# Making all of w_out's factors inside the h stage of the second MoE, and other due times for the attention steps, in a fused attention and two-MoE kernel on one Trainium2 core

## The chip, the cores and the metric

The kernel runs on one core of one Trainium2 chip, as one launch. The time is in device microseconds (us). The engines are TensorE (PE, matmuls; PEld is its weight load), VectorE (DVE), ScalarE (ACT), GpSimd (POOL) and SyncE (SP), which here issues every transfer. Each engine works through its own list of instructions in order. When an instruction waits, everything behind it on that engine waits too.

## The reference, cut to what matters

```python
q, k, v: (4, 8, 576, 64)            # batch, heads, sequence, head size
scores = where(mask, q @ k.T / 8, -1e9)   # heads 0-3: the last 32 keys; heads 4-7: every 32nd key
x  = softmax(scores) @ v                  # -> 2304 tokens x 512
h  = x @ w_in                             # first MoE, 512 -> 2048
x2 = (h * sigmoid(1.702 * h)) @ w_out     # 2048 -> 512
h2 = x2 @ w_in2                           # second MoE
out = (h2 * sigmoid(h2)) @ w_out2         # 2304 x 512
```

All inputs and the output are float32.

## The kernel before, in words

**Tiling.** The 2304 tokens are 8 chunks of 288 (half a sequence each). For every chunk there is an attention, then an h run of 16 groups (one for each 128 columns of w_in; a group is 12 matmuls of 288 columns), a gelu on each, then a g run of 16 groups of the same size against w_out. Matmuls are in fp16. Each float32 operand is split in a high and a low half, and a product takes three matmuls (high-high, high-low, low-high). Splitting takes two instructions: ACT or POOL writes the high half, and DVE's scalar_tensor_tensor then writes the low one.

**The second MoE** uses a Strassen-like form with 7 products in place of 8 for each pair of 2x2 blocks. It runs on whole pieces of 512 tokens (four, and one of 256), first all of h2 = x2 @ w_in2 ("the h stage", 18 blocks of 7 products, PE lines L1183), then the output ("the out stage", 18 blocks, L1294). For this both weight matrices have to be turned into 7 forms, called factors. w_in2 and w_out2 each give 8 batches. A batch loads two 128x512 tiles (A and B) from a scratch in HBM, makes two tiles U and V from them with four adds of 128x256, and splits the results in high and low halves: 5 high halves and 5 low halves for w_out2.

**Two planners.** Each instruction (or a short group) is a task with engines that may run it, a due time (its priority, in planned us) and buffers that it takes from named pools. A list scheduler in Python runs the tasks on modelled costs and writes down the resulting order for each engine. So a due time is no time on the chip: it decides the order on the queues, and nothing else. The first planner covers all but the last chunk; `PERIOD = 57` planned us separate chunk starts. The second covers chunk 7 (its h and g runs, L1013 and L1032), the h stage and the out stage.

**The attention of chunk c** runs within chunk c-1. `ATT` gives the due time of each step from that chunk's start: loads of q and v; sums of squares for the scale; the scale; the splits of q, k and v; then four head pairs (`s` for the first, `step` between them): scores on PE (L654 and L673), row maxima on DVE (L682), exps on ACT (L701), the normalising products on POOL (L719), transposes on PE (L726), their split (ACT L739, DVE L743); and last the products with v (`av`, L775) and the split of x (ACT L805, DVE L808). The gelu of the h run (L865) and the exp (L701) need different tables in ACT, so each change from one to the other loads a table.

**w_in2's factors** (`factors(0, i, ...)`, 8 batches) are made within the first planner, due at 245 + 22 i, and are stored to the scratch `in_factors`; the second planner loads them into the tile wf. **w_out2's factors** are made in two places. Three batches (`WO_EARLY`) come in the first planner, due at 415 + 20 i. Five come in chunk 7, due at 4 + 7 i (`factors_out`). All are stored to the scratch `out_factors` (L542, L1112) from buffers of the pool "f", and loaded from there during the h stage into regA and regB (L1120), where the out stage reads them. The pool "f" of the second planner has four buffers. It also serves each h block for the three factors that the block makes of its own result (L985) and stores with the rest of h2 (L1200, scratch `g_scratch`).

**An h block** runs 7 products into four PSUM banks of eight; ACT copies the first bank out (L1214) and applies silu to the second (L1223). DVE adds the other five results (L1190), ACT applies silu to those (L1195), and POOL or DVE makes the three factors (L985). L1214 of a block waits for the factors of the block two before it. The x2 pieces are loaded (L1144, L1146), added (L985) and split (L980 or L982, L992) in the same way, one piece ahead.

Helpers that all of this passes through have one line each: L385 and L387 (high halves, ACT and POOL) and L392 (low halves) in the first planner, L980, L982 and L992 in the second, L507 for the batch adds of the first planner, L295 and L290 for converting the parked weights.

## Time and profile before

| | us |
|---|---|
| median of 3 runs | 906.48 (902.98 to 908.37) |
| the profiled execution | 902.06 |
| its span on the core | 899.9 |
| PE busy in the span | 855.9 (95%) |
| DVE, ACT, POOL busy | 673.0, 591.0, 415.6 |
| HBM read and written | 107.74 MB and 60.82 MB |

The profiled execution is one run with the hardware profiler, and its own time is 2.2 us above its span. PE is busy for 95% of the span, so the time that an engine other than PE spends matters only where PE waits for it. The whole of PE's idle time is 44 us.

### The profile page before, as it was taken

How to read it: one execution, taken by the hardware profiler on the slowest of the kernel's cores; microseconds unless marked ns; L12 is line 12 of the kernel's file. 1: busy time of each engine (PE TensorE's matmuls, PEld its weight loads, DVE VectorE, ACT ScalarE, POOL GpSimd, SP SyncE). 2: the span in 40 equal slices, each digit the busy share in tenths (PEclk: the TensorE clock that was granted, in tenths of full speed). 3: DMA queues.
4: the chain of work that ended last, by engine and by line, in shares of the span. 5: the costliest groups of instructions: out<-in, count | busy, mean ns of one | idle time of the engine just before them, and what ended most of it. 6: DMA issues, size and time to landing. Idle time of an engine off the chain costs nothing.

```text
span 899.9 us, 21584 instructions
## 1 busy us (share of the span) xinstructions
PE 855.9 (95%) x8198; PEld 722.9 (80%) x8198; DVE 673.0 (75%) x1208; ACT 591.0 (66%) x1406; POOL 415.6 (46%) x426
## 2 busy tenths in 40 slices
PE   5999887999999899989999999989999999999997
PEld 4877675787887787777788788878888998888886
DVE  3799788987758788988668396768666489977852
ACT  5789588999969978879779464344444377555430
POOL 4667564453431445656337285556555242312110
PEclk9999999999999999999999999999999999999999
DMA  9857342464337376456413396888786669765611
GB/s 314 263 168 229 107 128 96 128 180 171 104 100 224 102 223 197 134 169 190 137 60 113 112 395 220 259 302 273 261 279 224 206 228 310 249 217 181 213 41 47
DMA packets 101319, 169.96 MB, mean 189 GB/s; under 512 B 9312, under 2 KB 58976, under 8 KB 100192
## 3 DMA queue, kind: packets, MB, share of 16 engines
q1 hardware_dynamic: 101216, 168.60, 57.9%
q8 instruction: 64, 1.05, 0.5%
q14 instruction: 39, 0.32, 0.1%
HBM read 107.74 MB, written 60.82 MB: 187 GB/s over the span
## 4 chain that ended last, share of the span: by engine, by line
PE 66%; DVE 13%; ACT 11%; DMA 4%; issue 3%; POOL 3%; SPq 0%; DVEq 0%; POOLq 0%; ACTq 0%
PE aps L1183 9%; PE aps L1294 9%; PE hps L1183 5%; PE gps L1183 4%; PE gps L888 4%; PE gps L1294 4%; PE hps L1294 3%; PE aps L857 3%; PE hps L888 3%; PE aps L888 3%; ACT sms L701 2%; ACT sml L701 2%; PE gps L857 2%; PE hps L857 2%; DVE wm L290 1%
## 5 line engine op out<-in xcount | busy, mean ns | idle before, releaser
L1183 PEld LDWEIGHTS <-wf 128*128 128x128 f16 x1680 | 151.2, 98 | 20.4 <-issue 4.5
L1294 PEld LDWEIGHTS <-wf 128*128 128x128 f16 x1512 | 147.8, 98 | 19.1 <-issue 1.6
L857 PEld LDWEIGHTS <-regA 128*128 128x128 f16 x1152 | 112.9, 99 | 41.8 <-issue 10.3
L985 POOL TENSOR_TENSOR tt<-tt 128x256 f32<-128x256 f32 (+2 forms) x102 | 89.0, 889 | 100.7 <-ACT tt L1195 22.0
L888 PEld LDWEIGHTS <-regB 128*128 128x128 f16 x1152 | 109.1, 98 | 29.0 <-issue 2.1
L857 PE MATMUL aps<-x,regA 128*128 128x288 f16 x576 | 76.8, 286 | 2.3 <-DVE g L392 1.4
L295 POOL TENSOR_TENSOR wm<-wm 128x512 int32<-128x512 int32 x32 | 42.5, 1328 | 69.2 <-DVE wm L290 40.0
L980 ACT ACTIVATE wf<-tt,xsg 128x512 f16<-128x512 f32 x86 | 56.9, 712 | 22.3 <-DMA tt<-g_scratch 8.5
L1294 PE MATMUL aps<-regA,wf 128*128 128x256 f16 x600 | 68.3, 273 | 1.4 <-DVE tt L1309 0.9
L992 DVE SCALAR_TENSOR_TENSOR wf<-tt,xsg,wf 128x512 f16<-128x512 f32 x86 | 68.5, 844 | 0.0
L719 POOL TENSOR_TENSOR sml<-sml,sus 96x384 f32<-96x384 f32 x32 | 30.3, 947 | 66.1 <-DVE sus L710 49.6
L888 PE MATMUL aps<-g,regB 128*128 128x288 f16 x432 | 58.1, 286 | 1.4 <-ACT sml L701 1.4
L1195 ACT ACTIVATE tt<-tt 128x512 f32<-128x512 f32 x35 | 22.0, 629 | 47.5 <-DVE tt L1190 42.7
L888 PE MATMUL gps<-g,regB 128*128 128x288 f16 x384 | 51.5, 286 | 0.8 <-ACT sms L701 0.8
L857 PE MATMUL gps<-x,regA 128*128 128x288 f16 x324 | 45.5, 292 | 7.0 <-DVE g L392 5.9
L1183 PE MATMUL aps<-xfa,wf 128*128 128x256 f16 (+1 forms) x444 | 46.6, 262 | 4.3 <-DVE x L1190 4.3
L888 PE MATMUL hps<-g,regB 128*128 128x288 f16 x336 | 45.7, 286 | 0.0
L539 DVE SCALAR_TENSOR_TENSOR wm<-wm,s 128x512 f16<-128x512 f32 (+1 forms) x47 | 41.0, 888 | 3.9 <-POOL wm L387 2.9
L1183 PE MATMUL aps<-g,wf 128*128 128x256 f16 x360 | 42.7, 273 | 0.0
L387 POOL TENSOR_SCALAR wm<-wm,s 128x512 f16<-128x512 f32 (+1 forms) x31 | 25.6, 833 | 25.5 <-issue 10.2
L980 ACT ACTIVATE wf<-regB,xsg 128x512 f16<-128x512 f32 x40 | 27.4, 712 | 13.7 <-PE hps L1294 3.8
L857 PE MATMUL hps<-x,regA 128*128 128x288 f16 x252 | 34.1, 286 | 1.6 <-DVE wm L290 1.6
(368 smaller groups left out, 2157.1 us busy)
## 6 DMA issues: line engine op xcount, KB each, us to landing
tt<-g_scratch SPq DMA_DIRECT2D x72, 256.0 KB, 4.0
g_scratch<-tt SPq DMA_DIRECT2D x62, 256.0 KB, 3.0
w<-in_moe_w_out_dram SPq DMA_DIRECT2D x24, 512.0 KB, 3.7
regB<-g_scratch SPq DMA_DIRECT2D x36, 256.0 KB, 4.2
rv<-in_v_dram SPq DMA_DIRECT2D x8, 1024.0 KB, 5.1
regB<-in_moe_w_in_dram SPq DMA_DIRECT2D x16, 512.0 KB, 8.2
w<-in_moe_w_in_dram SPq DMA_DIRECT2D x16, 512.0 KB, 3.7
w_scratch<-wm SPq DMA_DIRECT2D x32, 256.0 KB, 2.8
```

Of the source, the lines that this page charges most:

```text
L295: nc.gpsimd.tensor_tensor(out=di, in0=m.bitcast(I32), in1=di, op=ALU.add)
L387: nc.gpsimd.tensor_scalar(out=out, in0=in_, scalar1=s, scalar2=1.0, op0=ALU.mult, op1=ALU.mult)
L539: k = P.add(dve_t(256 * w), prio, lambda on, O=O, src=src: nc.vector.scalar_tensor_tensor(out=O()[:, 1], in0=src(), scalar=sc[nm][0], in1= ...
L701: nc.scalar.activation(out=sm[0:nq, e * nk:e * nk + nk], in_=bank[0:nq, (e % 4) * nk:(e % 4) * nk + nk], func=AF.Exp, bias=nms[0:nq, sl.id ...
L719: nc.gpsimd.tensor_tensor(out=smv(), in0=smv(), in1=sus[0:nq, sl.idx, 3 * g:3 * g + nb, None].to_broadcast([nq, nb, nk]), op=ALU.mult), [k ...
L857: nc.tensor.matmul(o, lhsT=pvA[:, f, x, kk, :], rhs=x1[:, y, kk, :], start=(i == 0), stop=(i == 3 * KD - 1))
L888: nc.tensor.matmul(o, lhsT=pvB[:, f, u, dt * 128:(dt + 1) * 128], rhs=g1[:, w, f, :], start=(f == 0 and j == 0), stop=(f == KF - 1 and j = ...
L980: nc.scalar.activation(out=out, in_=in_, func=AF.Copy, scale=s)
L985: return P.add({e: x for e, x in any_add(n).items() if e in by}, prio, lambda on: (nc.gpsimd if on == "POOL" else nc.vector).tensor_tensor ...
L992: dve_t(n), prio, lambda on: nc.vector.scalar_tensor_tensor(out=lo(), in0=src(), scalar=s(), in1=hi(), op0=ALU.mult, op1=ALU.subtract),
L1183: nc.tensor.matmul(place(b, f), lhsT=wf[:, nf * g + f, x, wa, 128 * kk:128 * kk + 128], rhs=rhs.rearrange("p (h t) -> p h t", h=2) if n2 = ...
L1294: nc.tensor.matmul(bank(b)[:, 256 * half:256 * half + 256], lhsT=fb[:, x, a, 128 * f:128 * f + 128], rhs=wt[:, 4 * p + f, z, wi, :], start ...
```

## The change

All 8 batches of w_out2's factors are made by the second planner in the h stage, one each 18 planned us, and their halves are written straight into regA and regB; `out_factors` and its stores and loads are gone. Each batch takes the four buffers of a new pool "w" (the former pool "r", in regB's rear, free once chunk 7's g run has read regB). These four go on to the out stage's pool "y" only after the last batch, where the pool "r" went there at the end of chunk 7. The batches of w_in2 come each 26 planned us in place of 22. And the attention steps of chunks 2 to 7 are due 8 planned us earlier, with 6 us in place of 5 between head pairs, and 4 to 5 us earlier for the products with v.

```diff
-FACT = ((245.0, 22.0), (415.0, 20.0))
-WO_EARLY = 3
-WO_LATE = (4.0, 7.0)
+FACT = (250.0, 26.0)
...
-ATT = {"load": (-20.0, -13.0), "square": (-8.0, 0.0), "scale": 2.0, "split": (6.0, 7.0, 16.0), "s": 22.0, "step": 5.0,
-       "av": (36.0, 49.0)}
+ATT = {"load": (-28.0, -20.0), "square": (-16.0, -8.0), "scale": -6.0, "split": (-2.0, 0.0, 10.0), "s": 14.0, "step": 6.0,
+       "av": (32.0, 44.0)}
...
-    for n, dst in enumerate((wfs, wos)):
-        for i in range(KF // 2 if n == 0 else WO_EARLY):
-            factors(n, i, FACT[n][0] + FACT[n][1] * i, k_w2[n], dst)
+    for i in range(KF // 2):
+        factors(i, FACT[0] + FACT[1] * i, k_w2[0])
...
     def factors_out(i, prio):
 
-        a, b, u, v = (P.buf("t") for _ in range(4))
+        a, b, u, v = (P.buf("w") for _ in range(4))
...
-        ka = P.dma(prio - 8, 0.25, lambda on: nc.sync.dma_start(out=A(), in_=w2s[1, i]), [x for z in late[:-1][-1:] for x in z], [a, u, v])
+        ka = P.dma(prio - 8, 0.25, lambda on: nc.sync.dma_start(out=A(), in_=w2s[1, i]), g_mm, [a, b, u, v], at=prio - 10)
...
-            o = P.buf("f")
-            O = lambda o=o, w=w: sl(o).bitcast(F16).rearrange("p (h e) -> p h e", h=2)[:, :, 0:256 * w]
-            h = P.add(any_hi(256 * w), prio, lambda on, O=O, src=src: put(on, O()[:, 0], src(), sc["wo"][0]), deps, [o], [x])
-            k = P.add(dve_t(256 * w), prio, lambda on, O=O, src=src: nc.vector.scalar_tensor_tensor(
-                out=O()[:, 1], in0=src(), scalar=sc["wo"][0], in1=O()[:, 0], op0=ALU.mult, op1=ALU.subtract),
-                [h], (), [x, o], two=True)
-            k_out[i].append(P.dma(prio + 2, 0.125 * w, lambda on, O=O, m=m, w=w: nc.sync.dma_start(
-                out=wos[i, :, :, m:m + w, :].rearrange("p h m e -> p h (m e)"), in_=O()), [k], (), [o]))
...
+            w = [lambda h=h, t=t, m=m, n=n: t[:, i, h, m:m + n, :].rearrange("p m e -> p (m e)") for h in range(2)]
+            out.append(halves(prio, 256 * n, w[0], w[1], src, lambda: sc["wo"][0], deps, [x]))
+        return out
+
+    wo = [factors_out(i, B0 + 14 + 18 * i) for i in range(8)]
...
-    P.add({"SP": 0.0}, 1e6, lambda on: None, g_mm, [P.buf("r", "y") for _ in range(4)])
+    P.add({"SP": 0.0}, 1e6, lambda on: None, g_mm, [P.buf("r", "w") for _ in range(4)])
+    P.add({"SP": 0.0}, 1e6, lambda on: None, [k for x in wo for k in x], [P.buf("w", "y") for _ in range(4)])
```

`B0` is the planned end of chunk 7, and `g_mm` its last g groups.

What the change moves on the queues is read from the order of the instructions. Lines after the change stand a little lower: L1188, L1197, L1169, L968, L1174, L1118, L1120 and L1026 are the old L1214, L1223, L1195, L980, L1200, L1144, L1146 and L1038; in the first planner L854, L690, L383, L820, L429 and L281 are L865, L701, L385, L831, L431 and L283.

**ACT, at the start of the h stage, before.** `tt<-tt,s` are high halves of the last two w_out2 batches, `g_78<-tt,s` those of an x2 piece.

```order
L1214 ACTIVATE tt<-aps,xih_6622 128x512
L980 ACTIVATE tt<-tt,s 128x256
L1214 ACTIVATE tt<-aps,xih_6622 128x512
L980 ACTIVATE g_78<-tt,s 128x512
L980 ACTIVATE g_78<-tt,s 128x256
L980 ACTIVATE tt<-tt,s 128x256 x2
L1223 ACT_TABLE_LOAD
L1223 ACTIVATE tt<-aps,xih_6622 128x512 x2
```

The same place after the change, where `regA<-regB,s` are high halves of the first w_out2 batch:

```order
L1188 ACTIVATE tt<-aps,xih_6559 128x512
L968 ACTIVATE g_78<-tt,s 128x512
L1188 ACTIVATE tt<-aps,xih_6559 128x512
L968 ACTIVATE g_78<-tt,s 128x512
L968 ACTIVATE regA<-regB,s 128x256
L968 ACTIVATE g_78<-tt,s 128x512
L968 ACTIVATE regA<-regB,s 128x512
L1169 ACT_TABLE_LOAD
```

The halves that have to wait for a buffer of the pool "f" are gone from between L1214 and the silus; halves of a batch still stand there, and now write where nothing has to be stored first.

**SP, at the start of the h stage, before.** `g_scratch<-` are the stores of h2.

```order
L1112 DMA out_factors<-tt 256x1x256 x2
L1200 DMA g_scratch<-tt 128x256
L1112 DMA out_factors<-tt 256x1x512
L1112 DMA out_factors<-tt 256x1x256
L1200 DMA g_scratch<-tt 128x256
L1112 DMA out_factors<-tt 256x1x512
L1112 DMA out_factors<-tt 256x1x256
L1200 DMA g_scratch<-tt 128x2x256 x2
L1120 DMA regA<-out_factors 128x2x1024
```

SP after the change, where `regB<-w_scratch` are a batch's two loads into the pool "w":

```order
L1118 DMA tt<-x_scratch 128x512
L1081 DMA regB<-w_scratch 128x512
L1120 DMA tt<-x_scratch 128x512
L1082 DMA regB<-w_scratch 128x512
L1174 DMA g_scratch<-tt 128x2x256
L1174 DMA g_scratch<-tt 128x256 x2
L1174 DMA g_scratch<-tt 128x2x256 x2
...
L1174 DMA g_scratch<-g_78 128x2x256
L1081 DMA regB<-w_scratch 128x512
```

No factor store stands among the h2 stores; instead the two loads of each later batch stand among them, and the first of the two waits there until the batch before it has left the pool "w".

**ACT, where chunk 4's g run passes into chunk 5's h run, before.** `g_78<-gps,sg` are high halves of a gelu, `wm<-wm,s` those of a w_in2 batch.

```order
L385 ACTIVATE wm<-wm,s 128x512
L865 ACT_TABLE_LOAD
L865 ACTIVATE gps<-gps,invh 128x288
L831 ACTIVATE ts<-hps,invg 128x288
L385 ACTIVATE g_78<-gps,sg 128x288
L865 ACTIVATE gps<-gps,invh 128x288
L701 ACT_TABLE_LOAD
L701 ACTIVATE sml,sus<-hps,nms,sc 96x128
L385 ACTIVATE g_78<-gps,sg 128x288
L431 ACTIVATE wm<-w_110 128x512
L865 ACT_TABLE_LOAD
```

The same place after:

```order
L690 ACTIVATE sml,sus<-gps,nms,sc 96x128 x3
L690 ACTIVATE sms,sus<-gps,nms,sc 72x72 x4
L854 ACT_TABLE_LOAD
L854 ACTIVATE aps<-aps,invh 128x288 x2
L383 ACTIVATE g_78<-aps,sg 128x288 x2
L429 ACTIVATE wm<-w_110 128x512
L854 ACTIVATE hps<-hps,invh 128x288
L281 ACTIVATE wm<-w_110 128x512
L383 ACTIVATE g_78<-hps,sg 128x288
L820 ACTIVATE ts<-hps,invg 128x288
```

The last exps of the attention now come before the first gelu, with one table load in place of three, and the batch halves stand elsewhere. Over the whole list up to chunk 7, ACT has 25 loads of the exp and gelu tables in place of 29.

## Rows read from the trace of the kernel before

**Rows 1.** The page, busy us of each engine, its share of the span, instructions.

```profile
PE 855.9 (95%) x8198; PEld 722.9 (80%) x8198; DVE 673.0 (75%) x1208; ACT 591.0 (66%) x1406; POOL 415.6 (46%) x426
```

**Rows 2.** Windows by stage: length, busy PE, PEld, DVE, ACT, POOL, clock, DMA.

```profile
137.30:205.40 68.10, 61.05 (x587) 48.58 (x587) 60.06 (x114) 61.39 (x162) 31.73 (x29) 0.97 0.44 137
205.40:509.60 304.20, 293.87 (x3118) 240.16 (x3116) 231.68 (x478) 248.05 (x672) 138.77 (x134) 1.00 0.47 145
509.60:556.80 47.20, 47.20 (x388) 37.73 (x387) 36.08 (x61) 24.16 (x50) 33.20 (x42) 1.00 0.87 314
556.80:725.60 168.80, 164.52 (x1636) 148.44 (x1634) 112.98 (x176) 70.62 (x119) 86.62 (x113) 0.99 0.75 246
725.60:899.90 174.30, 168.42 (x1564) 150.46 (x1561) 127.73 (x192) 84.74 (x136) 41.67 (x23) 1.00 0.57 189
```

**Rows 3.** Timeline of PE: start, length, instruction, in brackets idle before and releaser.

```profile
145.25 3.03 PE L857 MATMUL gps<-x,regA 128*128 128x288 f16 x12 [2.71 <-DVE g L392]
...
297.54 0.44 PE L726 MATMUL hps<-idt,sml 96*128 96x96 f32 x3 [1.42 <-DVE ptt L743]
...
397.32 1.63 PE L857 MATMUL gps<-x,regA 128*128 128x288 f16 x12 [1.20 <-DVE g L392]
...
400.25 1.63 PE L857 MATMUL gps<-x,regA 128*128 128x288 f16 x12 [1.29 <-DVE g L392]
...
430.61 0.76 PE L775 MATMUL hps<-ptt,vz 128*128 128x96 f16 x14 [0.96 <-DVE ptt L743]
...
588.90 2.72 PE L1183 MATMUL aps<-xfa,wf 128*128 128x256 f16 x12 [4.28 <-DVE x L1190]
591.41 1.70 PE L1183 MATMUL gps<-g,wf 128*128 128x256 f16 x12
...
752.01 1.47 PE L1294 MATMUL aps<-regA,wf 128*128 128x256 f16 x12 [0.92 <-DVE tt L1309]
```

**Rows 4.** Timelines of ACT, POOL and DVE ahead of PE's wait at 588.90.

```profile
569.91 0.51 ACT L980 ACTIVATE tt<-tt,s 128x256 f16<-128x256 f32 x1 [6.83 <-DMA out_factors<-tt]
...
577.48 7.30 POOL L985 TENSOR_TENSOR tt<-tt 128x256 f32<-128x256 f32 x8 [3.35 <-DMA out_factors<-tt]
...
585.09 0.72 ACT L980 ACTIVATE g<-tt,s 128x512 f16<-128x512 f32 x1 [2.96 <-DVE tt L985]
...
585.85 2.33 DVE L992 SCALAR_TENSOR_TENSOR g<-tt,s,g 128x512 f16<-128x512 f32 x2
...
586.64 1.25 ACT L1214 ACTIVATE tt<-aps,xih 128x512 f32<-128x512 f32 x2
...
588.11 0.74 DVE L1190 SCALAR_TENSOR_TENSOR x<-aps,xih,tt 128x512 f32<-128x512 f32 x1
```

**Rows 5.** DMA issues: transfer, count, size each, median us to landing.

```profile
tt<-w_scratch SPq DMA_DIRECT2D x9, 256.0 KB, 4.6
...
out_factors<-tt SPq DMA_DIRECT2D x15, 128.0 KB, 4.8
```

**Rows 6.** Timelines of POOL and ACT ahead of PE's waits at 397.32 and 400.25.

```profile
386.06 7.31 POOL L507 TENSOR_TENSOR wm<-wm 128x256 f32<-128x256 f32 x4
...
393.40 0.72 ACT L385 ACTIVATE wm<-wm,s 128x512 f16<-128x512 f32 x1 [2.81 <-POOL wm L507]
...
397.10 1.28 ACT L701 ACT_TABLE_LOAD   x1
```

**Rows 7.** Windows of line L1109 alone: length, busy DVE (instructions), clock, DMA.

```profile
509.60:556.80 47.20, 12.49 (x15) 1.00 0.87 314
...
556.80:725.60 168.80, 6.60 (x10) 0.99 0.75 246
```

**Rows 8.** Line L1109: count, shortest, median and longest in ns, first and last start, shapes.

```profile
L1109 DVE SCALAR_TENSOR_TENSOR tt<-tt,s x21: 473/745/1214, 515.5 to 570.5; 128x256 f16<-128x256 f32 x13, 128x512 f16<-128x512 f32 x8
```

**Rows 9.** Groups of instructions from 509 to 580: count, busy us, mean ns, idle before.

```profile
L985 POOL TENSOR_TENSOR tt<-tt 128x256 f32<-128x256 f32 x26 | 22.7, 894 | 26.3 <-DMA tt<-w_scratch 15.6 <-DMA out_factors<-tt 3.3 <-DMA tt<-x_scratch 3.0
...
L980 ACT ACTIVATE tt<-tt,s 128x512 f16<-128x512 f32 x5 | 3.5, 709 | 0.0
```

More of the change, by code (lines that the diff above doesn't have):

```diff
@@ L220, in attention_moe_moe2_kernel @@
     x2s = nc.dram_tensor("x2_scratch", (KD, 128, NT), F32, kind="Internal").ap()
-    wfs, wos = (nc.dram_tensor(f"{nm}_factors", (KF // 2, 128, 2, 7, 256), F16, kind="Internal").ap() for nm in ("in", "out"))
+    wfs = nc.dram_tensor("in_factors", (KF // 2, 128, 2, 7, 256), F16, kind="Internal").ap()
     w2s = nc.dram_tensor("w2_scratch", (2, KF, 128, 512), F32, kind="Internal").ap()
@@ L510, in attention_moe_moe2_kernel, with factors @@
     fed = [None]
[L512 to L514 removed]
+    def factors(i, prio, k_s):
         a, b, u, v = (P.buf("f") for _ in range(4))
         A, B, U, V = (lambda x=x: wm[:, x.idx] for x in (a, b, u, v))
[L517 to L518 removed]
+        ka = P.dma(prio - 8, 0.25, lambda on: nc.sync.dma_start(out=A(), in_=w2s[0, i]), [k_s, k_parked[0, i], fed[0]], [a, b], at=prio - 12)
+        kb = P.dma(prio - 8, 0.25, lambda on: nc.sync.dma_start(out=B(), in_=w2s[0, i + 8]), [ka, k_parked[0, i + 8]], (), [b])
         lo = lambda X: lambda: X()[:, 0:256]
         hi = lambda X: lambda: X()[:, 256:512]
[L521 to L533 removed]
+        k1 = any_add(prio, lo(U), lo(B), hi(B), ALU.add, [kb], [u, v], [b])
+        k3 = any_add(prio, lo(V), lo(A), lo(B), ALU.subtract, [ka, kb, k1], (), [v, a, b])
+        k2 = any_add(prio, hi(U), lo(U), lo(A), ALU.subtract, [k1, ka], (), [u, a])
+        k4 = any_add(prio, hi(V), hi(A), hi(U), ALU.subtract, [k2, k3], (), [v, a, u])
+        parts = ((a, A, 0, 2, [ka]), (b, hi(B), 2, 1, [kb]), (u, U, 3, 2, [k1, k2]), (v, V, 5, 2, [k3, k4]))
         fed[0] = k1
@@ L1088, in attention_moe_moe2_kernel @@
         out=wf[:, i].rearrange("p h m e -> p (h m e)"), in_=wfs[i].rearrange("p h m e -> p (h m e)")), at=4.5 * i)] for i in range(8)]
-    k_out, late = {}, []
     def factors_out(i, prio):
-        a, b, u, v = (P.buf("t") for _ in range(4))
+        a, b, u, v = (P.buf("w") for _ in range(4))
         A, B, U, V = (lambda x=x: sl(x) for x in (a, b, u, v))
-        ka = P.dma(prio - 8, 0.25, lambda on: nc.sync.dma_start(out=A(), in_=w2s[1, i]), [x for z in late[:-1][-1:] for x in z], [a, u, v])
-        kb = P.dma(prio - 8, 0.25, lambda on: nc.sync.dma_start(out=B(), in_=w2s[1, i + 8]), [x for z in late[:-1][-1:] for x in z], [b])
+        ka = P.dma(prio - 8, 0.25, lambda on: nc.sync.dma_start(out=A(), in_=w2s[1, i]), g_mm, [a, b, u, v], at=prio - 10)
@@ L1097, in factors_out @@
+        kb = P.dma(prio - 8, 0.25, lambda on: nc.sync.dma_start(out=B(), in_=w2s[1, i + 8]), [ka], (), [b])
         lo = lambda X: lambda: X()[:, LO]
         hi = lambda X: lambda: X()[:, HI]
-        k1 = add_up(prio, 256, lo(U), hi(A), lo(A), ALU.subtract, [ka], (), [u, v, a])
-        k3 = add_up(prio, 256, lo(V), hi(B), hi(A), ALU.subtract, [k1, kb], (), [v, a, b])
+        k1 = add_up(prio, 256, lo(U), hi(A), lo(A), ALU.subtract, [ka], (), [u, a])
+        k3 = add_up(prio, 256, lo(V), hi(B), hi(A), ALU.subtract, [ka, kb], (), [v, a, b])
@@ L1115, in attention_moe_moe2_kernel @@
-    for i in range(WO_EARLY, 8):
-        factors_out(i, WO_LATE[0] + WO_LATE[1] * (i - WO_EARLY))
-        late.append(k_out[i])
-    wo = []
-    for i in range(8):
-        wo.append([P.dma(B0 + 20 + 15 * i + e, 0.46, lambda on, i=i, w=w, m=m: nc.sync.dma_start(
-            out=w[:, i].rearrange("p h m d -> p h (m d)"), in_=wos[i, :, :, m].rearrange("p h m d -> p h (m d)")), [*g_mm, *k_out.get(i, [])], at=B0 + 5 + 15 * i)
-            for e, (w, m) in enumerate(((woa, slice(0, 4)), (wob, slice(4, 7))))])
+        out = []
@@ new lines, in factors_out @@
+        for x, src, t, m, n, deps in ((a, lo(A), woa, 0, 1, [ka]), (b, B, woa, 1, 2, [kb]), (v, lo(V), woa, 3, 1, [k3]),
+                                      (u, U, wob, 0, 2, [k1, k2]), (v, hi(V), wob, 2, 1, [k4])):
+            w = [lambda h=h, t=t, m=m, n=n: t[:, i, h, m:m + n, :].rearrange("p m e -> p (m e)") for h in range(2)]
+            out.append(halves(prio, 256 * n, w[0], w[1], src, lambda: sc["wo"][0], deps, [x]))
+        return out
+    wo = [factors_out(i, B0 + 14 + 18 * i) for i in range(8)]
```

28 lines of the change are left out of this document (4 added, 24 removed).

## The prediction

> **What bounds the kernel now.** I read the page first: PE is busy for 855.9 of 899.9 us [rows 1], so the whole kernel follows PE, and what a change off PE can win or lose is a share of the 44 us in which PE is idle. The windows by stage say where these lie [rows 2]. The stretch of chunk 1's attention and h run loses 68.10 - 61.05 = 7.05 us, the five chunks after it 304.20 - 293.87 = 10.33, chunk 7 nothing, the h stage 168.80 - 164.52 = 4.28, the out stage 5.9. The rest, 16.5 us, is the start, which the change does not reach. In the same rows DVE is the next engine: 60.06 of 68.10 in the first stretch, 231.68 of 304.20 in the chunks, 112.98 of 168.80 in the h stage.
>
> Then the timeline of PE, for the waits themselves [rows 3]. The h stage's whole loss is one wait: 4.28 us before 588.90, for an L1190 of DVE. The matmuls behind it are slow too: 2.72 us for twelve that take 1.47 elsewhere, then 1.70. The chunks lose in many small pieces: twice a gelu half (L392), twice the split of transposed scores (L743), 0.96 to 1.42 us each. Of each wait I looked at what stood ahead of its releaser on the other engines.
>
> For 588.90 that is plain [rows 4]. ACT stood for 6.83 us until 569.91, because a high half of a late w_out2 batch had no buffer: the store of an earlier half had not landed. POOL stood for 3.35 us until 577.48 for the same kind of store, and did eight adds after that. So the block factors and an x2 piece came late, ACT waited 2.96 us more for that piece, its L1214 went out at 586.64, and DVE's L1190 behind two L992 at 588.11; PE began 0.8 us later. A store of this kind takes 4.8 us to land [rows 5], and four buffers serve these stores and the h blocks.
>
> For 397.32 and 400.25 it is a batch of w_in2's factors [rows 6]: four adds on POOL took 7.31 us from 386.06, ACT stood 2.81 us for one of them with a high half at the head of its queue, and the first gelu of chunk 5, the change of table and the first gelu halves all stood behind it. Right after, at 397.10, ACT changed its table back for one exp, 1.28 us.
>
> **The change part by part.** The sum is made against the profiled execution's own 902.06 us, which is 4.4 us (0.5%) below the median of 906.48; at the end I scale by the ratio.
>
> *The late batches leave chunk 7.* PE has no idle time there [rows 2], so their 12.49 us of DVE in chunk 7 and 6.60 in the first blocks [rows 7] are worth nothing in themselves. Worth something is that no store of theirs holds a buffer of the pool "f" any more. With it goes the wait of 4.28 us, and the slow matmuls behind it: 2.72 - 1.47 = 1.25 and 1.70 - 1.47 = 0.23. Together -5.76 us. The bounds are 0 (another delay of the same blocks takes its place) and -5.76; I take all of it, since both waits that began the chain name these stores. What is late next is the first w_out2 batch. Its loads can go out only when chunk 7's g run is done with regB; one takes 4.6 us [rows 5], and its first half stands behind the second block's L1214, some 9 us on, so they are covered.
>
> *Eight batches enter the h stage.* Five late batches cost DVE 12.49 + 6.60 = 19.09 us of low halves [rows 7], so 3.82 each and 30.5 for eight. DVE then has 112.98 - 6.60 + 30.5 = 136.9 us in a stage of 164.5 (83%). ACT gets at most 32 high halves at 0.709 [rows 9], 22.7 us on 70.62, and POOL 27 adds at 0.894, 24.1 on 86.62. None is full: the cover is PE itself, and the out stage runs with 127.73 of DVE in 174.30 with a largest wait of 0.92 us in the rows shown [rows 2, 3]. What remains is order: a high half waits at the head of ACT for a POOL add, and L1214, L1223 and the silus wait behind it. That is the mechanism of 397.32. It cost PE 1.20 + 1.29 = 2.49 us in one of eleven batches of the first planner, 0.23 us a batch, so I take 8 x 0.23 = +1.8 us. The bounds are 0 and 8 x 2.49 = 19.9.
>
> *SP.* 40 stores and 16 loads go, 16 loads from w_scratch stay. A batch's first load waits on SP until the batch before has left its buffers, with h2 stores behind it; if a batch is late by some us, these stores are too, and with them buffers of "f". That is the same price as above by another door, and I keep it in the same bounds. The out stage's first loads can use regB's rear only after the last batch; they find the x2 pieces' buffers first, so I cost it at nothing; without that cover it is one load, 4.6 us by the nearest row [rows 5].
>
> *Attention due 8 earlier, and eight batches in place of eleven in the chunks.* The instructions stay the same but for four table loads (5.1 us of ACT at 1.28 [rows 6]) and the three batches, 3 x 3.82 = 11.5 us of DVE out of 231.68. PE's waits in the chunks come from collisions, which a new order removes and makes anew. The order shows chunk 4's last exps ahead of the first gelu with one table load in place of three, so the 2.49 us of 397.32 and 400.25 should go. The transposes stand about as close ahead of the products with v as before, so waits like 297.54 and 430.61 will go in one place and come in another; the lighter DVE is worth a little. I take -3.0 us. The bounds are -10.33 (all idle time of the chunks) and +7.05 (a second loss like that of chunk 1, which has much the fullest DVE).
>
> Sum: -5.76 + 1.8 - 3.0 = -6.96, so 895.10; 895.10 / 902.06 x 906.48 = **899.5 us**.
>
> **A rule against this change.** The rows first: the shortest low half of 256 took 0.473 us, while the median of the late batches was 0.745 and the longest 1.214 [rows 8], and POOL's adds beside them took 0.894 us on average [rows 9]. The Trainium skill ("SBUF — State Buffer", Who interferes with whom) says that a DVE instruction with two SBUF inputs and a GpSimd instruction that reads SBUF share a port pair as an exclusive lock, so that the second to come blocks until the first has finished. The trace agrees that such pairs stretch. If each of the 40 low halves waited for a whole add, DVE would spend 24 x 0.473 + 16 x 0.745 + 40 x 0.894 = 59.0 us on them in place of 30.5, have 165.4 in the stage, and be its bound: some 2.4 us over PE's 163.0, and the sum -4.5, which is 902 us, an estimate by that page. By the rows it is 30.5, since the late batches already ran among such adds.
>
> **The rivals.**
>
> *The batches hold up the h stage (slower).* Place: ACT in the h stage, a high half before L1223 or L1214, waiting for an add on POOL that low halves of DVE have stretched. For it: rows 6 show the like, and the new order puts halves of a batch between these lines in every second block. Against it: PE can run most of a block ahead in PSUM, and in the h stage before only stores of factors, and no adds, began the long wait [rows 4]. At 2.49 us a batch it is +19.9 - 5.76 - 3.0 = +11.2, which is 917.7 us. It decides from (5.76 + 3.0) / 8 = 1.1 us a batch on. The lock above would make it likelier; that sentence changes no number here.
>
> *The chunks give the gain back (no change).* The exps now fall within the h runs, where ACT also has the gelus; if this makes waits like those of chunk 1 [rows 2, 3], +7.05 - 5.76 + 1.8 = +3.1, so 909.6 us.
>
> *The chunks run through (faster still).* All 10.33 us go and the batches cost nothing: -16.1, so 890.3 us. For it: earlier attention lets the next chunk's h groups start between the last g groups. Against it: the waits of the chunks are of several kinds [rows 3], and one new order hardly cures all of them.
>
> That the change does not do what it says is excluded by the order.
>
> **How the numbers follow.** Forecast 0.50, with a range of its own of 894.5 to 905 (chunks 0 to -6, batches 0 to 4); slower rival 0.18; gain given back 0.20; all of the chunks' idle time gone 0.12. A measurement of this kernel tells no less than 0.5%, 4.5 us, from no change: below 902 is faster, above 911 slower. Of the forecast some 0.12 lies above 902, of the slower rival a part below 911. So faster 0.50, same 0.30, slower 0.20. The range leaves out most of the slower rival and little else: 889.5 to 912.
>
> **What would show it.** Right: no idle time of PE near the third and fourth blocks of the h stage, and PE at full clock there; no ACT or POOL wait for a factor store; DVE near 137 us in the h stage; PE idle near 7 us in the chunks 2 to 6. Wrong: waits of PE for L1190 every second block with ACT idle for POOL ahead of them, an SP that waits at a batch's load, or more than 10 us of PE idle time between chunk 2 and chunk 7.

## The result, and the profile after

The kernel after takes 894.77 us (median of 5 runs, 893.69 to 898.02), the kernel before 906.48 us in the same session (5 runs, 902.14 to 908.37). The ratio is 0.9888, with a 95% interval from 0.9851 to 0.9925: faster by about 10 us. A second session gave 0.9892 (0.9857 to 0.9927). The time lies inside the predicted range, 4.7 us below the forecast.

The profiled execution is the one of 898.02 us, the slowest of the five. The page's first part, which answers to [rows 1]:

```profile
PE 860.5 (96%) x8198; PEld 726.8 (81%) x8198; DVE 666.8 (74%) x1192; ACT 588.2 (66%) x1414; POOL 420.5 (47%) x430
```

PE is busy 4.6 us longer than before, with the same matmuls, in a span that is 3.7 us shorter. So some matmuls ran slower, and a stage table is needed to see where. These are the windows of the kernel after, with the columns of [rows 2]: chunks 1 to 6, chunk 7, the h stage up to the first matmul of the out stage, and from the start of the h stage to the end.

```profile
142.42:511.17 368.75, 355.84 (x3703) 289.73 (x3703) 279.02 (x566) 299.49 (x830) 160.18 (x147) 0.99 0.43 133
511.17:558.34 47.17, 47.17 (x386) 37.72 (x386) 21.81 (x47) 17.24 (x35) 19.43 (x27) 1.00 0.56 211
558.34:719.94 161.60, 161.60 (x1612) 146.39 (x1610) 133.08 (x201) 83.87 (x145) 116.78 (x147) 1.00 0.69 221
558.34:896.20 337.86, 331.37 (x3196) 298.08 (x3193) 261.48 (x391) 169.43 (x280) 157.44 (x169) 1.00 0.63 204
```

The same windows of the kernel before, for chunks 1 to 6 and from the h stage to the end:

```profile
137.30:509.60 372.30, 354.92 (x3702) 288.74 (x3702) 291.75 (x591) 309.44 (x833) 170.50 (x163) 1.00 0.46 144
...
556.80:899.90 343.10, 332.93 (x3196) 298.90 (x3193) 240.70 (x367) 155.35 (x254) 128.29 (x135) 0.99 0.66 217
```

Read the lengths first. From the h stage to the end it is 343.10 - 337.86 = 5.24 us less; PE's idle time there falls from 10.17 to 6.49 and its busy time by 1.56. Chunk 7 is the same (47.20 and 47.17). Chunks 1 to 6 are 3.55 us shorter. And the stretch before chunk 1's h run, where the order of instructions is the same in both kernels, took 142.42 us in place of 137.28. So 8.8 us were gained in the changed stages, and this one execution lost 5.1 us in code that the change does not touch (the last section says how). In the chunks PE's idle time fell from 17.38 to 12.91 us (length less busy time), while its busy time rose by 0.92.

In the h stage PE has no idle time at all. What is left of waits on PE's timeline in the changed stages, of 1 us and more from chunk 2 on, answers to [rows 3]:

```profile
221.45 0.38 PE L643 MATMUL gps<-mB,idb 72*72 72x126 bf16 x4 [1.05 <-DVE wm L288]
230.60 1.63 PE L846 MATMUL aps<-x,regA 128*128 128x288 f16 x12 [2.25 <-ACT sml L690]
...
353.47 0.44 PE L715 MATMUL aps<-idt,sml 96*128 96x96 f32 x3 [1.05 <-DVE g L390]
355.62 3.04 PE L877 MATMUL aps<-g,regB 128*128 128x288 f16 x12 [1.12 <-DVE g L390]
...
749.24 1.47 PE L1268 MATMUL hps<-regA,wf 128*128 128x256 f16 x12 [1.50 <-DVE x L1283]
```

The 4.28 us of 588.90 and the two waits for gelu halves near 400 [rows 3] are gone; an exp (L690) holds up chunk 2 for 2.25 us, where PE had no wait at all. Exps held PE up before as well, in chunks 1, 3, 4 and 6, for at most 1.37 us (timeline of PE, the kernel before):

```profile
350.80 1.39 PE L888 MATMUL aps<-g,regB 128*128 128x288 f16 x10 [1.37 <-ACT sml L701]
```

Together PE's waits for exps in chunks 2 to 6 come to 2.5 us after and 3.4 before.

The low halves of the w_out2 batches, which answer to [rows 7, 8], are these groups of DVE in the h stage (shape, count, busy us, mean ns of one, idle before):

```profile
L980 DVE SCALAR_TENSOR_TENSOR regA<-regB,s,regA 128x256 f16<-128x256 f32 x16 | 10.4, 651 | 0.0
...
L980 DVE SCALAR_TENSOR_TENSOR regA<-regB,s,regA 128x512 f16<-128x512 f32 x8 | 7.8, 976 | 0.2 <-ACT regA L968 0.2
...
L980 DVE SCALAR_TENSOR_TENSOR regB<-regB,s 128x512 f16<-128x512 f32 x8 | 6.9, 864 | 0.0
...
L980 DVE SCALAR_TENSOR_TENSOR regB<-regB,s 128x256 f16<-128x256 f32 x8 | 4.3, 544 | 0.0
```

Together they are 10.4 + 7.8 + 6.9 + 4.3 = 29.4 us for 40.

PE waits for none of this work, but ACT does. It stands at high halves of batches until their loads land, nine times in the h stage, 3.2 us at the longest (view of the waits of ACT: us in total, times, longest):

```profile
ACT regA L968 <- DMA regB<-w_scratch: 9.4, 9, 3.2
```

### The profile page after: what moved, and what is told of

It is laid out like the page before. It is cut to its first block, busy times and chain, and to the rows that moved or that the text cites. A ratio compares the mean times of both kernels' runs of the same rounds, so it can differ in the third digit from the quotient of the medians.

```text
span 896.2 us, 21423 instructions
## 1 busy us (share of the span) xinstructions
PE 860.5 (96%) x8198; PEld 726.8 (81%) x8198; DVE 666.8 (74%) x1192; ACT 588.2 (66%) x1414; POOL 420.5 (47%) x430
## 3 DMA queue, kind: packets, MB, share of 16 engines
q8 instruction: 64, 1.05, 0.5%
## 4 chain that ended last, share of the span: by engine, by line
PE 58%; ACT 14%; DVE 13%; DMA 6%; issue 5%; POOL 3%; SPq 0%; DVEq 0%; POOLq 0%; ACTq 0%
PE aps L1157 9%; PE aps L1268 8%; PE hps L1157 5%; PE gps L1157 4%; PE aps L877 4%; PE hps L1268 4%; PE gps L1268 4%; PE hps L877 2%; ACT sms L690 2%; ACT sml L690 2%; ACT g L383 2%; DMA rk<-in_k_dram 1%; DVE g L390 1%; ACT jk L488 1%; PE gps L1020 1%
## 5 line engine op out<-in xcount | busy, mean ns | idle before, releaser
L973 POOL TENSOR_TENSOR tt<-tt 128x256 f32<-128x256 f32 (+2 forms) x84 | 75.1, 903 | 45.0 <-ACT tt L1169 11.6
L877 PE MATMUL aps<-g,regB 128*128 128x288 f16 x576 | 79.6, 289 | 1.1 <-DVE g L390 1.1
L293 POOL TENSOR_TENSOR wm<-wm 128x512 int32<-128x512 int32 x32 | 47.6, 1490 | 57.9 <-DVE wm L288 36.3
L968 ACT ACTIVATE wf<-tt,xsg 128x512 f16<-128x512 f32 x87 | 58.1, 712 | 24.9 <-PE hps L1268 7.5
L980 DVE SCALAR_TENSOR_TENSOR wf<-tt,xsg,wf 128x512 f16<-128x512 f32 x87 | 71.5, 869 | 0.0
L1268 PE MATMUL aps<-regA,wf 128*128 128x256 f16 x456 | 53.2, 273 | 0.1
L1157 PE MATMUL aps<-xfa,wf 128*128 128x256 f16 (+1 forms) x528 | 53.1, 256 | 0.0
L1169 ACT ACTIVATE tt<-tt 128x512 f32<-128x512 f32 x39 | 24.4, 625 | 29.6 <-DVE tt L1164 29.5
L846 PE MATMUL gps<-x,regA 128*128 128x288 f16 x288 | 39.5, 289 | 2.9 <-DVE g L390 2.3
L968 ACT ACTIVATE wf<-regB,xsg 128x512 f16<-128x512 f32 x39 | 26.9, 714 | 21.9 <-POOL regB L973 7.1
L877 PE MATMUL gps<-g,regB 128*128 128x288 f16 x288 | 38.7, 286 | 0.3 <-ACT sms L690 0.3
L877 PE MATMUL hps<-g,regB 128*128 128x288 f16 x288 | 38.8, 286 | 0.0
L1268 PE MATMUL aps<-regB,wf 128*128 128x256 f16 x312 | 37.0, 273 | 0.0
L390 DVE SCALAR_TENSOR_TENSOR g<-aps,sg,g 128x288 f16<-128x288 f32 x48 | 24.2, 510 | 14.1 <-ACT g L383 13.9
```

Source lines behind the costliest of these rows:

```text
L293: nc.gpsimd.tensor_tensor(out=di, in0=m.bitcast(I32), in1=di, op=ALU.add)
L390: dve_t(n), prio, lambda on: nc.vector.scalar_tensor_tensor(out=lo(), in0=src(), scalar=s(), in1=hi(), op0=ALU.mult, op1=ALU.subtract),
L846: nc.tensor.matmul(o, lhsT=pvA[:, f, x, kk, :], rhs=x1[:, y, kk, :], start=(i == 0), stop=(i == 3 * KD - 1))
L877: nc.tensor.matmul(o, lhsT=pvB[:, f, u, dt * 128:(dt + 1) * 128], rhs=g1[:, w, f, :], start=(f == 0 and j == 0), stop=(f == KF - 1 and j = ...
L968: nc.scalar.activation(out=out, in_=in_, func=AF.Copy, scale=s)
L973: return P.add({e: x for e, x in any_add(n).items() if e in by}, prio, lambda on: (nc.gpsimd if on == "POOL" else nc.vector).tensor_tensor ...
```

## The experiments

Ratios are to the kernel before in the same session, with 95% intervals; us are medians. "Idle" is PE's idle time, summed over the brackets of its timeline, which leave out gaps under 0.15 us (by length less busy time the sums are up to 0.6 us higher). Chunks 1 to 6 run from chunk 1's first h matmul to chunk 7's.

| kernel | us | ratio | until chunk 1 | chunks 1 to 6 | idle in chunks 1, 2, 3, 4, 5, 6 | h stage to end |
|---|---|---|---|---|---|---|
| before | 906.48 | 1 | 137.3 | 372.3 | 7.06, 0, 3.06, 2.13, 4.18, 0.76 | 343.1 |
| after | 894.77 | 0.9888 (0.9851 to 0.9925) | 142.4 | 368.8 | 2.59, 4.11, 0.60, 2.79, 1.24, 1.05 | 337.9 |
| hstage_only | 897.24 | 0.9914 (0.9890 to 0.9939) | 139.7 | 371.2 | 7.04, 0, 3.21, 1.53, 4.15, 0.16 | 337.6 |
| att_only | 906.69 | 1.0014 (0.9990 to 1.0038) | 143.1 | 374.4 | 1.98, 4.16, 0.61, 4.24, 2.83, 2.64 | 343.2 |
| old_att | 891.16 | 0.9845 (0.9819 to 0.9871) | 141.9 | 364.3 | 7.02, 0, 3.91, 0.81, 0, 0 | 336.8 |
| no_late_stores | 901.33 | 0.9965 (0.9944 to 0.9987) | 137.3 | 373.3 | 7.03, 0, 3.91, 1.77, 4.28, 0.75 | 342.0 |
| mixed | 892.48 | 0.9859 (0.9838 to 0.9880) | 139.7 | 368.4 | 2.80, 0.61, 4.59, 4.13, 0.29, 0 | 336.9 |
| start245 | 896.51 | 0.9925 (0.9902 to 0.9948) | 139.2 | 369.8 | 6.59, 0, 3.18, 2.20, 0.66, 0 | 336.9 |
| dense | 911.59 | 1.0077 (1.0054 to 1.0099) | 139.3 | 369.8 | 3.30, 4.45, 0.58, 2.88, 0.62, 1.06 | 354.9 |
| dense14 | 908.80 | 1.0053 (1.0029 to 1.0078) | 140.8 | 368.5 | 3.30, 3.96, 0.42, 2.88, 1.38, 1.07 | 350.6 |
| adds_dve | 898.98 | 0.9935 (0.9914 to 0.9956) | 140.9 | 369.5 | 3.29, 4.03, 0.61, 2.54, 0.82, 1.06 | 342.2 |
| after_again | 895.81 | 0.9892 (0.9857 to 0.9927) | 142.1 | 371.4 | 3.30, 4.53, 0.61, 3.43, 1.34, 1.07 | 337.7 |
| old_att_again | 889.83 | 0.9835 (0.9806 to 0.9863) | 137.9 | 363.6 | 5.89, 0, 3.11, 0.73, 0, 0.16 | 336.8 |
| park125 | 891.61 | 0.9857 (0.9829 to 0.9885) | 140.4 | 365.0 | 6.06, 1.83, 0, 2.70, 0, 0.75 | 337.3 |

**hstage_only: the move of w_out2's factors alone.**

```diff
-FACT = (250.0, 26.0)
+FACT = (245.0, 22.0)
...
-ATT = {"load": (-28.0, -20.0), "square": (-16.0, -8.0), "scale": -6.0, "split": (-2.0, 0.0, 10.0), "s": 14.0, "step": 6.0,
-       "av": (32.0, 44.0)}
+ATT = {"load": (-20.0, -13.0), "square": (-8.0, 0.0), "scale": 2.0, "split": (6.0, 7.0, 16.0), "s": 22.0, "step": 5.0,
+       "av": (36.0, 49.0)}
```

> The kernel after with the due times of attention and of w_in2's batches as before, so that only the move of w_out2's batches is left. First theory (the two parts add up): PE's wait near the third h block is gone and nothing takes its place, so from the start of the h stage to the end it is about 5 us shorter than before, and the chunks are nearly as before, but for three batches fewer: 5 to 7 us faster in all. Rival (the w_out2 batches are nearly the whole effect, by way of the three batches that leave the chunks): 9 to 11 us faster, with PE's idle time in the chunks as low as in the kernel after. Rival (the due times are the whole effect): within 2 us of before.

8.6 thousandths faster, some 7.8 us; the interval, 5.5 to 10 us, takes in most of the first theory's 5 to 7 us and reaches into the 9 to 11 of the second. But the second wanted the idle time in the chunks as low as in the kernel after, and the trace shows 5.5 us of gain from the h stage on and 1.1 us in the chunks, where little changes. PE's waits between 390 and 440 us (us in total, times, longest) are still those of the kernel before:

```profile
PE gps L846 <- DVE g L390: 3.2, 3, 1.3
PE hps L764 <- DVE ptt L732: 0.9, 1, 0.9
```

**no_late_stores: the kernel before without the stores of the late batches.**

```diff
-            k_out[i].append(P.dma(prio + 2, 0.125 * w, lambda on, O=O, m=m, w=w: nc.sync.dma_start(
-                out=wos[i, :, :, m:m + w, :].rearrange("p h m e -> p h (m e)"), in_=O()), [k], (), [o]))
+            k_out[i].append(k)
...
-            out=w[:, i].rearrange("p h m d -> p h (m d)"), in_=wos[i, :, :, m].rearrange("p h m d -> p h (m d)")), [*g_mm, *k_out.get(i, [])], at=B0 + 5 + 15 * i)
+            out=w[:, i].rearrange("p h m d -> p h (m d)"), in_=wos[i % 3, :, :, m].rearrange("p h m d -> p h (m d)")), [*g_mm, *k_out.get(i, [])], at=B0 + 5 + 15 * i)
```

> The kernel before without the 25 stores of the five late w_out2 batches; the loads of these five take the factors of the three early ones, so part of the output is computed from other factors, and 3.3 MB are not written. High and low halves, the loads and all due times stay. First theory (the stores held the buffers of the pool f, and that began the wait of 4.28 us): no wait of ACT or POOL for a factor store, PE has no wait over 1 us in the first six h blocks, and the kernel is 4 to 6 us faster than before. Rival (five batches of halves in chunk 7 and the first blocks are simply too much work for ACT, POOL and DVE there): the halves come later into the h blocks as before, PE waits 3 us or more near the third or fourth block, and the kernel is within 2 us of before.

Its waits of PE from the start of the h stage to the end, all of them:

```profile
PE aps L1293 <- DVE wf L992: 1.3, 1, 1.3
PE gps L1057 <- DVE cs L1055: 1.3, 1, 1.3
PE hps L1293 <- DVE tt L1308: 1.3, 2, 0.9
```

The wait of 4.28 us is gone with the stores alone, though the halves of five batches are all still made. [rows 8] has 21 of the 25 low halves; the other four begin from 571.3 on, the last at 574.4. Without the stores the last of all 25 begins at 562.2 (the first line is of the kernel before, the second of this one):

```profile
L1109 DVE SCALAR_TENSOR_TENSOR tt<-g,s,tt x3: 472/740/908, 572.2 to 574.4; 128x256 f16<-128x256 f32 x2, 128x512 f16<-128x512 f32 x1
L1109 DVE SCALAR_TENSOR_TENSOR tt<-tt,s x25: 472/907/1211, 516.5 to 562.2; 128x256 f16<-128x256 f32 x15, 128x512 f16<-128x512 f32 x10
```

No ACT or POOL wait for a factor store is left between 540 and 600 us. So the stores made the halves late, not the amount of work. Two small waits came new, 1.28 us for a scale at 564.49, among the first blocks where the first theory allowed none over 1 us, and 1.34 for a split in the out stage. So the gain is 3.2 us by the ratio (1.2 to 5.1), a little under the 4 to 6 expected.

**att_only: the new due times of attention in the kernel before.**

```diff
-ATT = {"load": (-20.0, -13.0), "square": (-8.0, 0.0), "scale": 2.0, "split": (6.0, 7.0, 16.0), "s": 22.0, "step": 5.0,
-       "av": (36.0, 49.0)}
+ATT = {"load": (-28.0, -20.0), "square": (-16.0, -8.0), "scale": -6.0, "split": (-2.0, 0.0, 10.0), "s": 14.0, "step": 6.0,
+       "av": (32.0, 44.0)}
```

> The kernel before with the attention's new due times alone. First theory: the chunks are some 3 to 5 us shorter and the wait before the third h block is as before (4 us), so 3 to 5 us faster. Rival (the lighter load of batches is what shortens the chunks): within 2 us of before. Rival (new collisions of exps and gelus in the h runs): 3 us or more slower.

No difference, which is what the first rival named. Chunk 1 loses 5 us of idle time, chunks 2, 4 and 6 take on 4.2, 2.1 and 1.9, and chunks 3 and 5 give back 3.8. The two waits of 397.32 and 400.25 [rows 3] are gone here too: from 390 to 445 us PE waits for a gelu half (L392) for 0.2 us only. PE's waits from 205 to 262 us, where the kernel before has none:

```profile
PE aps L857 <- ACT sml L701: 2.3, 1, 2.3
PE gps L654 <- DVE wm L290: 1.2, 1, 1.2
PE gps L775 <- DVE ptt L743: 0.7, 1, 0.7
```

**old_att: the kernel after with the old due times of attention.**

```diff
-ATT = {"load": (-28.0, -20.0), "square": (-16.0, -8.0), "scale": -6.0, "split": (-2.0, 0.0, 10.0), "s": 14.0, "step": 6.0,
-       "av": (32.0, 44.0)}
+ATT = {"load": (-20.0, -13.0), "square": (-8.0, 0.0), "scale": 2.0, "split": (6.0, 7.0, 16.0), "s": 22.0, "step": 5.0,
+       "av": (36.0, 49.0)}
```

> The kernel after with the attention's old due times, and w_in2's batches 26 planned us apart as in the kernel after. First theory: the h and out stages as in the kernel after, the chunks as before less a little, so 5 to 7 us faster than before, and within 1 us of the kernel that also has the old spacing of the batches. Rival (the wider spacing is what relieves the chunks): 3 us or more below that kernel.

The rival's number holds: 6.1 us below hstage_only, from which it differs by w_in2's batches alone (245 and 22 there, 250 and 26 here). PE has no wait at all between 390 and 440 us, where hstage_only has the four just shown. And its median is 3.6 us below that of the kernel after, though the intervals of the two ratios overlap.

**after_again and old_att_again: the two side by side, unchanged.**

> The kernel after, unchanged, beside the kernel with the attention's old due times in one session. First theory (the new due times cost the kernel after some 3 us, because the exps that now fall within chunk 2 keep PE waiting and one more stretch of half clock follows): a ratio to before of 0.987 to 0.991, and 2 to 5 us above the other. Rival (their difference was chance of the start's clock): within 1.5 us of each other.

> The kernel with the attention's old due times, unchanged, in the same session. First theory: a ratio to before of 0.983 to 0.987, and 2 to 5 us below the kernel after. Rival: within 1.5 us of it.

895.81 against 889.83: 6 us, the same way as the first pair (3.6 us). Chance alone is unlikely to give both, though single runs of the two still overlap (889.25 at the lowest, 893.51 at the highest). So the new due times cost this kernel some 4 to 6 us. In the two pairs of traces the chunks are 4.5 and 7.8 us longer by them, of which idle time is 0.6 and 4.4. Another 2.5 and 2.1 us come from matmuls at half clock: the chunks have 5.0 and 6.8 us of it with the new due times, none and 2.7 with the old.

**start245: the same distance of 26, five planned us earlier.**

```diff
-FACT = (250.0, 26.0)
+FACT = (245.0, 26.0)
```

> The kernel after with the attention's old due times and w_in2's batches due from 245 on, each 26 planned us: only the start differs by 5 planned us from the kernel that took 891.2 us. First theory (the distance of 26 between the batches is what takes the waits of 397 to 433 us away): no wait of PE over 0.5 us after 390 us, and 890 to 893 us. Rival (it is where single batches happen to fall among the gelus and exps): waits of 1 us and more come back in some of the chunks 3 to 6, and 894 to 898 us.

The rival's numbers hold: the ratio is back near that of hstage_only, with a new wait of 1.55 us at 382.95, in chunk 4. So the distance alone is not what helped old_att; its start of 250 belongs to it. The waits are a small part of the difference, though: in this trace the chunks hold only 0.9 us more idle time than in old_att's, and after 390 us a single wait of 0.66. The other 4.6 us are PE's busy time, with half clock for 3.4 us right behind 382.95 and for 5.0 us in chunk 1. That it matters where single batches fall among gelus and exps fits this, but which batch meets what was not taken apart.

**mixed: the new due times in chunk 1 only.**

```diff
-        tab = ATT0 if c == 0 else ATT1 if c == 1 else ATT
+        tab = ATT0 if c == 0 else ATT1 if c == 1 else ATT2 if c == 2 else ATT
```

Here `ATT2` is the new table and `ATT` the old one.

> The kernel after, with the new due times for the attention of chunk 2 alone (which runs within chunk 1) and the old ones for chunks 3 to 7. First theory (the new due times take away part of chunk 1's 7.0 us of idle time, and cost 4.1 us of it in chunk 2 and a stretch of half clock later; each effect stays with its own chunk): chunk 1 has 2 to 3 us of idle time, chunk 2 none, the later chunks as in the kernel with the old due times, so 886 to 889 us where that kernel took 891.2. Rival (any change of one chunk's order moves the collision on to the next chunk): chunk 2 or 3 has some 4 us of idle time, and it takes 891 us or more.

Chunk 1 and chunk 2 came near what the first theory has (2.80 and 0.61), but chunks 3 and 4 have 4.59 and 4.13 us of idle time, where old_att has 3.91 and 0.81: the rival. The 4.2 us saved in chunk 1 are given back, most of it in chunk 4, where the attention has its old due times. An effect does not stay with its chunk.

**park125: fewer conversions of weights in chunk 1.**

```diff
-PARK = (105.0, 9.0)
+PARK = (125.0, 8.0)
```

> The kernel with the attention's old due times, and the conversions of the second MoE's weights due from 125 on, each 8 planned us, in place of 105 and 9; so chunk 1, where DVE is fullest, has two or three of them fewer and the chunks behind it more. First theory (DVE's load in chunk 1 is what makes its 7.0 us of idle time): PE idle 2 to 4 us in chunk 1, and 3 to 5 us faster than the kernel with the old due times alone. Rival (the collision moves on to other chunks): chunk 1 gains and chunks 2 to 5 lose about the same, within 2 us of that kernel.

No gain over old_att. Chunk 1 keeps 6.06 us, of which a wait of 2.88 for POOL at 177.75 is new, and chunk 2 takes on 1.83; chunk 3 loses the 3.91 of old_att, and chunk 4 rises from 0.81 to 2.70. The sum is nearly the same: the rival.

**dense and dense14: w_out2's batches closer together in the h stage.**

```diff
-    wo = [factors_out(i, B0 + 14 + 18 * i) for i in range(8)]
+    wo = [factors_out(i, B0 + 14 + 9 * i) for i in range(8)]
```

and `14 * i` in the other.

> The kernel after with w_out2's eight batches due each 9 planned us in place of 18, so that all of them fall in the first half of the h stage. First theory (PE works ahead in PSUM and DVE has room, so the batches cost PE nothing): even at twice the rate PE waits 3 us or less in the h stage, so within 3 us of the kernel after, 895 to 898. Rival (the batches hold up the h stage; at 18 apart the cover is nearly used up): DVE over 95% in the first half of the stage, PE waits for DVE's additions from the results of the products, and 5 to 15 us slower than the kernel after.

> The kernel after with w_out2's batches each 14 planned us, between the 18 of the kernel after (no wait of PE in the h stage) and the 9 that made it 17 us slower with 13 us of waits there. First theory (a batch's load can go out only when the batch before has left its four buffers, and ACT stands at a high half until it lands; at 14 the load still lands in time): PE waits less than 2 us in the h stage, 894 to 898 us. Rival (18 is just at the edge, and the price grows in proportion to the density): PE waits 4 to 7 us, and 901 to 905 us.

In both the rival holds, and by more than it said: from the h stage to the end 17.0 and 12.7 us longer than the kernel after, 2.1 and 1.6 us a batch. Idle time of PE is 11.7 and 9.7 us of this, and the rest busy time: the traces have 10.2 and 6.8 us of half clock in the h stage, where the kernel after has none. In dense, DVE is at 96% in one stretch of 20 us and below that in the others, and POOL under 90% everywhere. So no engine is full over the stage, and what makes PE wait is order, as dense14's timelines of ACT, DVE and PE show ahead of its longest wait:

```profile
671.55 0.51 ACT L968 ACTIVATE regB<-regB,s 128x256 f16<-128x256 f32 x1 [3.73 <-POOL regB L973]
671.73 2.13 DVE L980 SCALAR_TENSOR_TENSOR regA<-regB,s,regA 128x256 f16<-128x256 f32 x3
671.97 0.67 ACT L1188 ACTIVATE tt<-aps,xih 128x512 f32<-128x512 f32 x1
...
673.78 1.33 DVE L980 SCALAR_TENSOR_TENSOR regB<-regB,s 128x512 f16<-128x512 f32 x2
...
675.04 0.74 DVE L1164 SCALAR_TENSOR_TENSOR tt<-aps,xih,tt 128x512 f32<-128x512 f32 x1
...
675.83 2.72 PE L1157 MATMUL aps<-xfa,wf 128*128 128x256 f16 x12 [5.35 <-DVE tt L1164]
```

A high half of a batch stands at the head of ACT for 3.73 us until POOL has done an add. Behind it is the copy of a block's first bank (L1188); on DVE five low halves of that batch then stand ahead of the addition (L1164) for which PE waits. In dense, ACT stands at a high half for a batch's load as well, in seven places and 18.0 us together, 5.8 us at the longest, twice what it does in the kernel after (view of the waits of ACT, up to 690 us):

```profile
ACT regA L968 <- DMA regB<-w_scratch: 18.0, 7, 5.8
```

**adds_dve: the adds of these batches bound to DVE.**

```diff
-        k1 = add_up(prio, 256, lo(U), hi(A), lo(A), ALU.subtract, [ka], (), [u, a])
+        k1 = add_up(prio, 256, lo(U), hi(A), lo(A), ALU.subtract, [ka], (), [u, a], by=("DVE",))
```

and so for all four.

> The kernel after with the 32 adds of w_out2's batches bound to DVE, which takes about 27 of them from POOL. First theory (the cover is PE itself): DVE rises from 133 to some 147 of 161.6 us in the h stage (91%), and PE still hardly waits; within 2 us of the kernel after. Rival (DVE is close to being the bound, and what it does in an exclusive turn with POOL makes it fuller): PE waits 3 us or more in the h stage. By the exclusive lock of the Trainium skill (SBUF - State Buffer, Who interferes with whom), POOL's reads gone, the low halves of the batches should come down from the 0.73 us that each took in the kernel after towards the shortest, 0.47 for 256 columns and 0.74 for 512.

Between the two theories. From the h stage to the end it takes 4.3 us more than the kernel after, with 2.6 us of waits in the h stage and one of 1.61 after it; but the interval of its ratio overlaps that of the kernel after. DVE rose by 7.2 us there (268.7 against 261.5) and not by 14: in the h stage the batches' adds brought 11.8 us, but DVE had 3.8 us less of the other adds. The low halves did not come down in sum, two groups fell and two rose; the same four groups sum to 9.0 + 6.5 + 7.8 + 6.6 = 29.9 us:

```profile
L980 DVE SCALAR_TENSOR_TENSOR regA<-regB,s,regA 128x256 f16<-128x256 f32 x16 | 9.0, 564 | 0.0
L980 DVE SCALAR_TENSOR_TENSOR regB<-regB,s 128x512 f16<-128x512 f32 x8 | 7.8, 977 | 0.0
L980 DVE SCALAR_TENSOR_TENSOR regB<-regB,s 128x256 f16<-128x256 f32 x8 | 6.6, 829 | 0.0
L980 DVE SCALAR_TENSOR_TENSOR regA<-regB,s,regA 128x512 f16<-128x512 f32 x8 | 6.5, 811 | 0.0
```

POOL still made the h blocks' own adds, beside 30 of these 40 low halves, so this doesn't show what they would cost with POOL idle.

## Why the prediction was right, and where its working failed

**The wait in the h stage (-5.76): right, place, size and cause.** From the h stage to the end 5.24 us went. PE's busy time fell by 1.56, where the slow matmuls were put at 1.48. The idle time fell by 3.68: the 4.28 went, and the out stage's idle time grew by 0.6, from 5.88 [rows 2] to 6.49. That the factor stores began it is shown by no_late_stores, where the wait and the half clock behind it are gone with the stores alone.

**Eight batches in the h stage (+1.8): too much, it was about nothing.** DVE came to 133.1 us where 136.9 was worked out, and 82% where 83% was; the 40 low halves to 29.4 where 30.5 was. PE waited for none of it, so the price of 0.23 us a batch, borrowed from the first planner, wasn't due. The prediction also has the first batch's loads covered; ACT waited 1.7 us for loads up to 600 us and 9.4 in the whole stage, so it was PE's own cover that held. But the cover is thinner than that 0 looks: the rival of the batches that hold up the h stage, by a high half at ACT's head that waits for an add, has been seen at work in dense14, at 1.6 us a batch where it was to decide from 1.1. At a distance of 18 planned us it is off, at 14 it is on.

**The lock: not by its size.** The rows gave 30.5 us for the 40 low halves, the estimate with a whole add ahead of each 59.0; 29.4 were measured. The shortest and longest of the regA group (count, shortest, median and longest in ns):

```profile
L980 DVE SCALAR_TENSOR_TENSOR regA<-regB,s,regA x24: 469/756/1233, 568.8 to 702.4; 128x256 f16<-128x256 f32 x16, 128x512 f16<-128x512 f32 x8
```

Of the 40, seven ran while POOL did nothing, and took 0.47 us for 256 columns and 0.74 for 512. The 33 that overlap POOL's work took 0.47 to 0.97 and 0.73 to 1.23. The Trainium skill ("SBUF — State Buffer", Who interferes with whom) has the two engines take turns; the trace agrees that low halves are stretched beside POOL, but not that each waits for a whole instruction of it: none took over 0.5 us longer than alone, and a batch's add on POOL took 0.81 on average (spans on POOL are rough).

**The chunks (-3.0): the sum came near by chance, the step failed.** Chunks 1 to 6 are 3.55 us shorter. The failing step is the -3.0 itself, which the prediction puts down to the attention's new order and three batches fewer, "so the 2.49 us of 397.32 and 400.25 should go". The two waits did go, and they go by that order alone (att_only); but as much comes in other places, so alone it gains nothing (1.0014). What the prediction put at nothing, without a reason, is the third part of the change, the new due times of w_in2's batches (from 250 on, each 26). With the attention's old order they take the same two waits away and are worth 6.1 us. By the lengths of the chunks in the table (one trace each, with what the clock did in it) the three parts, one after the other, are -1.1 us (three batches fewer, hstage_only), -6.9 (w_in2's due times, old_att) and +4.5 (the attention's new order, the kernel after). That these come near -3.0 is luck.

The price of the new order is only in part what the rival that gives the gain back names, exps within the h runs. PE waits for exps for 2.5 us in chunks 2 to 6, 2.25 of it at 230.60, and for 2.1 in old_att. New against old_att are 2.2 us more for gelu halves, 1.9 for converted weights (L288) and 1.0 for POOL's normalising products. Ahead of the late gelu halves of 350.79 to 355.62, ACT has eight exps between two changes of table (timeline of ACT, the kernel after):

```profile
343.95 1.28 ACT L690 ACT_TABLE_LOAD   x1
...
350.19 1.28 ACT L854 ACT_TABLE_LOAD   x1
```

So the rival's exps may be behind these too; that was not tested, and the cause of the other waits stays open.

The place was wrong as well: PE's idle time in chunks 2 to 6, foretold near 7 us, was 10.13 before and is 9.79 after (sums of the table); what fell was chunk 1's, from 7.06 to 2.59. By length less busy time the 9.79 is 10.1, and 11.3 in after_again, which is over the 10 us that the prediction names as a sign of being wrong.

**The three batches that left the chunks** are in hstage_only, and the chunks are 1.1 us shorter in its one trace.

**The total (899.5 against 894.77).** By stages the gain is 3.55 + 5.24 = 8.8 us, not 6.96: 1.3 of the difference is from the h stage on, 0.5 in the chunks. The rest, from 8.8 to 11.7, is within the interval of the ratio (6.8 to 13.5 us), and the start's clock spreads single runs by as much.

**A faster version came out:** old_att, with the attention's old due times and the rest of the change, 889.8 to 891.2 us, 0.9835 and 0.9845 of before.

## What to carry to other kernels

A wait of the bound engine that begins with a store holding a buffer is worth a change: look for what the waiting engines ahead of it name, and take the store out of the pool's way. Here, work moved under a busy TensorE was free only up to a spacing, and the cover ended by order (a half at the head of a queue), with every engine's average still below full; so try the spacing at two values before trusting the cover. Shifts of due times in a list-scheduled stretch mostly moved collisions from one place to another, so test each table of a change by itself: one part of a change that won as a whole was costing it 4 to 6 us, and a part that the prediction had not priced was worth 6.
